# A transformer block on one core: memory keys and shared keys earlier, second values later

## The chip, the cores and the metric

One core of a Trainium2 chip runs the whole program as one launch. The metric is device time in microseconds (us) of one execution, input in device memory to output in device memory; lower is better. The core has five engines with an instruction queue each, worked through in order: TensorE (PE; its weight loads are listed as PEld), VectorE (DVE), ScalarE (ACT), GpSimd (POOL) and SyncE (SP), which here issues nearly all transfers (DMAs). DMAs move data between device memory and the on-chip memories; PSUM is the memory into which TensorE writes, in eight banks.

## What is computed

Chunked attention with memory keys and values, and then a mixture of eight experts in which each token goes to one expert. Cut to what matters:

```python
# B, H, S, D = 4, 8, 768, 64; 8 memory rows a head; chunks of 32 queries
for c in range(S // 32):
    q_c   = q[:, :, c_start:c_start + 32]
    k_ctx = k[:, :, max(0, c_start - 16):min(S, c_end + 8)]   # left 16, own 32, right 8
    v_ctx = v[:, :, same rows]
    k_full, v_full = concat([mem_k, k_ctx]), concat([mem_v, v_ctx])
    a = softmax(q_c @ k_full.T / sqrt(D))
    out[:, :, c_start:c_end] = a @ v_full
x = out as 3072 tokens of 512
expert = argmax(x @ w_gate); gate = softmax of it
y = relu(x_e @ w1[e]) @ w2[e] for each expert's tokens (at most `capacity`), times gate
```

## The kernel before

**Tiling.** The attention goes through 12 segments of 256 tokens (four batches of three) and 24 tiles `t` of 128 tokens, two to a segment `n`. For a segment, `load_k` and `load_q` (L360, L352) bring keys and queries of all eight heads with two tokens to a partition; `trans_k` and `trans_q` transpose them on TensorE; ACT and DVE copy the result from PSUM into the key window `KW` and into `qT`. The window has, for each chunk, 64 columns: 24 keys that it shares with the chunk before it, 32 own ones, 8 memory keys; heads come in pairs, so that a head's 64 rows stand in a half `hf` of the partitions and the other half's columns must be zero. `copy_k` fills the shared columns: L492 puts the first keys of a batch (from `preT`) into the first chunk, L496 copies the last 24 own keys of each chunk into the next, L498 into the next segment's window. `fill_mem_k` (L450) fills the memory columns from `preT`, which `trans_pre` makes out of one load of `mem_k` (L118) and one of the first keys (L119). Values come in blocks `k` of two tiles: `load_v` (eight heads, eight transfers and one small one), `fill_mem_v` (two transfers from the tile `ME` that GpSimd assembles from `mem_v`), `copy_v` (L414, L415).

**A tile.** `scores(t)`: 16 products on TensorE (L509, listed as 32 matmuls), a maximum (L517) and a subtraction (L520) on DVE. `exps(t)` on ACT (L526), `trans_p`, `value` (L550 on TensorE, L553 to L558 on DVE), `trans_out`, `logits`, and later `route`. Key windows and value windows have two buffers each (`KW[n % 2]`, `VW[k % 2]`), the raw loads a ring of two.

**Order.** Nothing is scheduled by a planner: each engine runs its instructions in the order in which the program writes them, and waits where a tile is not ready. Ahead of the loop stand the first loads, `dummy(11)` (each unit listed as two matmuls, on zeros), the zeroing of the windows (`zero_k`, `zero_v`, L128 and L135, both from a zero tile or as memset; L173 for one half of `KW[1]`), the first segment's transposes and copies, `dummy(20)`, the memory rows, the loads of segment 2 and of value block 1. In the loop, tile `t` of even number does `fill_mem_k(n)`, `scores`, `trans_k(n)`, `load_k(n + 2)` for `n = t // 2 + 1`; the odd tile does `scores`, `trans_q(n)`, `load_q(n + 2)`; then value work of the tiles before. Value block 2 and later ones are loaded from t = 3 on.

**SP's queue before**, in order: keys 0 (two halves), queries 0 (two halves), `mem_k`, first keys, `mem_v` of batch 0 (two), keys 1, queries 1, values 0 (nine), fill 0 (two), keys 2, queries 2, fill 1 (two), values 1 (eight), then from the loop `mem_v` of batch 1, keys 3, `w_gate`, `mem_v` of batch 2, queries 3, `mem_v` of batch 3, keys 4, queries 4, values 2 and so on.

The experts follow from about 137 us on: PE-bound matrix products with the weights split into two parts.

Of the kernel before, what the change touches and what calls it, by code (L numbers as in the profile page):

```python
# [17 lines left out]
P = 128  # L18
# [11 lines left out]
NKW, NVW = 2, 2  # L30
# [20 lines left out]
class Kernel:  # L51
# [41 lines left out]
    def attention(self):  # L93
# [31 lines left out]

        def zero_k(i, hf):
            r = slice(hf * 64, hf * 64 + 64)
            nc.vector.tensor_copy(out=KW[i][r, :, :, 1 - hf, :].rearrange("p a c d -> p (a c) d"),  # L128
                                  in_=self.pad[r, None, 0:64].broadcast_to([64, 32, 64]))
# [9 lines left out]

        self.load_k(0)  # L140
        self.load_q(0)
        load_mem()
        load_memv(0)
# [13 lines left out]
        zero_v(0, 0, nc.scalar.copy)  # L157
        zero_v(0, 1, None)
        self.load_v(0)
        self.trans_k(0)  # L160
        self.trans_q(0)
        self.trans_pre(pre)
        dummy(20)
        self.copy_k(0)
        self.fill_mem_k(0)
        zero_k(1, 0)
        nc.gpsimd.memset(ME, 0.0)
        for par in range(2):
            nc.gpsimd.memset(ME[par * 32:par * 32 + 32, par, :, 64:65], 1.0)
        for par in range(2):  # L170
            r = slice(par * 32, par * 32 + 8)
            nc.gpsimd.tensor_copy(out=ME[r, par, :, 0:64], in_=memv[r])
        nc.gpsimd.memset(KW[1][64:P, :, :, 0, :].rearrange("p a c d -> p (a c) d"), 0.0)  # L173
        self.fill_mem_v(0)
        self.load_k(2)
        self.load_q(2)
        zero_v(1, 0, None)
        zero_v(1, 1, None)
        self.fill_mem_v(1)
        self.load_v(1)  # L180
        self.okd = False
# [6 lines left out]
        for t in range(NTL):  # L188
# [12 lines left out]
            if n < NS:  # L201
                if t % 2 == 0:
                    self.trans_k(n)
                    if n + 2 < NS:
                        self.load_k(n + 2)
                else:
                    self.trans_q(n)
                    if n + 2 < NS:
                        self.load_q(n + 2)
            self.exps(t)  # L210
            if 0 <= t - 1 < NTL:
# [217 lines left out]
    def trans_pre(self, src):  # L429
# [5 lines left out]
        for j in range(2):  # L435
            for hf in range(2):
                nc.scalar.copy(out=self.preT[hf * 64:hf * 64 + 64, :, j::2, :].rearrange("p a r c -> p (a r) c"),
                                      in_=ps[j * 64:j * 64 + 64, hf::2].rearrange("p (a c) -> p a c", a=8))

# [3 lines left out]
    def fill_mem_k(self, n):  # L443
# [4 lines left out]
        for hf in range(2):  # L448
            r = slice(hf * 64, hf * 64 + 64)
            (self.nc.scalar.copy if n == 0 and not hf else (self.nc.gpsimd if n and not hf else self.nc.vector).tensor_copy)(  # L450
                out=kw[r, :, :, hf, 56:64], in_=self.pre_cols(0, b)[r, :, None, :].broadcast_to([64, 4, 8, 8]))
# [16 lines left out]
    def trans_k(self, n):  # L468
        nc = self.nc
        kw = self.KW[n % NKW]  # L470
        src = self.kn.pop(n)
        for hf in range(2):
            ps = self.psum().rearrange("p (h t) -> p h t", h=4)
            for i in range(4):
                nc.tensor.transpose(out=ps[:, i, :], in_=src[:, 2 * i + hf, :], identity=self.ident)
            ps = ps.rearrange("p h (m t) -> p h m t", t=16)
# [7 lines left out]
    def copy_k(self, n):  # L484

        nc = self.nc
        b, s = self.segs[n]
        kw, kx = self.KW[n % NKW], self.KW[(n + 1) % NKW]
        if s == 0:
            for hf in range(2):  # L490
                r = slice(hf * 64, hf * 64 + 64)
                nc.vector.tensor_copy(out=kw[r, :, 0, hf, 16:24], in_=self.pre_cols(1, b)[r])  # L492
        for hf in range(2):
# [560 lines left out]
```

## Time and profile before

| | us |
|---|---|
| median of 3 runs | 485.65 |
| the three runs | 484.39, 485.65, 493.61 |
| the profiled execution, its own time | 483.69 |
| span of the profiled execution, first to last instruction | 481.8 |
| busy in it: PE / DVE / ACT / POOL | 458.3 / 308.9 / 232.6 / 118.2 |

The 1.89 us between the span and the execution's own time lie around the program. Busy shares are means over an attention stage (to about 137 us) and an expert stage with different limits, so they are read by stage. A row of busy time by stretch gives the stretch, its length, the busy time of PE, PEld, DVE, ACT and POOL (each with the number of instructions), the clock granted to TensorE as a share of 2.4 GHz, the mean busy share of the sixteen DMA engines, and GB/s. A row of a timeline gives when a group of like instructions began, how long it lasted, engine, line, operation, out<-in with sizes, the count and, in brackets, how long the engine had sat idle before and what released it. An instruction that has been taken up but is blocked counts as busy, so an instruction that is longer than its twin tells of a wait.

### The profile page before, as it was taken

The numbers are of one execution on the slowest core, as the hardware profiler recorded it, in microseconds if no ns is written. First come the engines' busy times: TensorE is split into PE (matmuls) and PEld (weight loads), VectorE is DVE, ScalarE is ACT, GpSimd is POOL, SyncE is SP. The second block draws the span as 40 slices with busy tenths as digits, with TensorE's granted clock in tenths as the row PEclk, the third lists the DMA queues.
The fourth block names the chain that finished last, engine by engine and source line by source line (L and its number), as shares of the span: only waits on it lengthen the run. The fifth ranks groups of instructions, "written<-read, shape, count | busy, mean of one in ns | idle before, by whom it ended". The sixth has DMA issues, their size and how long they took to land.

```text
span 481.8 us, 11847 instructions
## 1 busy us (share of the span) xinstructions
PE 458.3 (95%) x4317; PEld 386.9 (80%) x4317; DVE 308.9 (64%) x686; ACT 232.6 (48%) x423; POOL 118.2 (25%) x158
## 2 busy tenths in 40 slices
PE   7899999999999999979999999999999999899993
PEld 6777877878789897867777898899888878677782
DVE  5988899999869447565448257555624676674410
ACT  6587968889635235255345056244502544533200
POOL 8631245555543621201001100100021011020011
PEclk9899999999999999999999999999999999999998
DMA  9787788897976755365705554270414356430011
GB/s 214 150 216 189 184 209 245 249 246 186 230 252 236 263 167 193 105 224 180 237 34 181 173 190 133 88 267 16 164 53 149 123 187 229 163 131 3 1 42 44
DMA packets 79920, 78.85 MB, mean 164 GB/s; under 512 B 33394, under 2 KB 60142, under 8 KB 79792
## 3 DMA queue, kind: packets, MB, share of 16 engines
q1 hardware_dynamic: 74992, 62.33, 44.4%
q0 software_dynamic: 4800, 14.95, 8.1%
q8 instruction: 65, 1.06, 1.0%
q14 instruction: 63, 0.52, 0.3%
HBM read 61.25 MB, written 15.99 MB: 160 GB/s over the span
## 4 chain that ended last, share of the span: by engine, by line
PE 52%; DMA 18%; issue 13%; DVE 10%; ACT 2%; SPq 1%; POOLq 1%; DVEq 0%; ACTq 0%
PE ps L858 19%; DMA out_dram<-y,tok 13%; PE ps L948 13%; PE lgp L927 5%; DMA raw<-in_q_dram 3%; PE ps L834 2%; PE ps L550 2%; DVE vw L415 2%; PE ps L463 2%; PE ps L509 2%; PE ps L331 2%; ACT kw L479 1%; DVE m L517 1%; DVE d L520 1%; SPq L397 1%
## 5 line engine op out<-in xcount | busy, mean ns | idle before, releaser
L871 ACT ACTIVATE hhi<-ps 128x512 fp32r<-128x512 f32 x68 | 40.7, 599 | 148.6 <-PE ps L858 133.0
L955 POOL DMA_INDIRECT out_dram<-y,tok x28 | 32.3, 1155 | 273.3 <-DVEq L842 140.9
L872 DVE SCALAR_TENSOR_TENSOR hlo<-ps,hhi 128x512 fp32r<-128x512 f32 x68 | 47.0, 691 | 68.6 <-ACT hhi L871 65.7
L858 PE MATMUL ps<-xhi,w1hi 128*128 128x320 f32 (+3 forms) x288 | 59.5, 328 | 3.6 <-ACT w2hi L849 1.7
L948 PE MATMUL ps<-w2hi,hhi 128*128 128x512 f32 x152 | 60.9, 401 | 0.0
L948 PE MATMUL ps<-w2lo,hhi 128*128 128x512 f32 x152 | 59.8, 393 | 0.0
L948 PE MATMUL ps<-w2hi,hlo 128*128 128x512 f32 x152 | 59.4, 391 | 0.0
L858 PE MATMUL ps<-xhi,w1lo 128*128 128x320 f32 (+3 forms) x288 | 57.7, 322 | 0.0
L858 PE MATMUL ps<-xlo,w1hi 128*128 128x320 f32 (+3 forms) x288 | 57.7, 322 | 0.0
L858 PEld LDWEIGHTS ps<-xhi,w1hi 128*128 128x128 f32 x288 | 45.2, 188 | 8.3 <-issue 2.1
L858 PEld LDWEIGHTS ps<-xhi,w1lo 128*128 128x128 f32 x288 | 45.9, 188 | 2.9
L858 PEld LDWEIGHTS ps<-xlo,w1hi 128*128 128x128 f32 x288 | 45.9, 188 | 2.8
L954 DVE TENSOR_SCALAR y<-ps,xg 128x512 f32<-128x512 f32 x19 | 14.3, 751 | 51.6 <-PE ps L948 44.0
L850 DVE TENSOR_TENSOR w2lo<-raw,w2hi 128x512 fp32r<-128x512 f32 x64 | 41.2, 685 | 0.9 <-DVEq L919 0.6
L823 DVE TENSOR_TENSOR w1lo<-raw,w1hi 128x512 fp32r<-128x512 f32 x56 | 36.7, 684 | 2.7 <-DVEq L842 0.8
L822 ACT CAST w1hi<-raw 128x512 fp32r<-128x512 f32 (+1 forms) x72 | 37.1, 573 | 0.9
L849 ACT CAST w2hi<-raw 128x512 fp32r<-128x512 f32 x64 | 36.2, 617 | 1.6 <-DMA raw<-in_moe_w_dram 1.6
L838 ACT CAST xhi<-ps 128x512 fp32r<-128x512 f32 x34 | 19.8, 587 | 29.6 <-PE ps L834 26.3
L948 PEld LDWEIGHTS ps<-w2hi,hlo 128*128 128x128 f32 x152 | 28.6, 188 | 6.7
L948 PEld LDWEIGHTS ps<-w2hi,hhi 128*128 128x128 f32 x152 | 28.5, 188 | 6.7
L839 DVE TENSOR_TENSOR xlo<-ps,xhi 128x512 fp32r<-128x512 f32 x34 | 23.1, 689 | 16.7 <-ACT xhi L838 16.7
L948 PEld LDWEIGHTS ps<-w2lo,hhi 128*128 128x128 f32 x152 | 28.5, 188 | 5.8
(169 smaller groups left out, 814.6 us busy)
## 6 DMA issues: line engine op xcount, KB each, us to landing
raw<-in_moe_w_dram SPq DMA_DIRECT2D x15, 2048.0 KB
raw<-in_q_dram SPq DMA_DIRECT2D x11, 512.0 KB
raw<-in_k_dram SPq DMA_DIRECT2D x10, 512.0 KB
vw<-in_v_dram SPq DMA_DIRECT2D x49, 64.0 KB
xg<-x_d SPq DMA_DIRECT2D x3, 792.0 KB
vw<-in_v_dram SPq DMA_DIRECT2D x31, 72.0 KB
xg<-x_d SPq DMA_DIRECT2D x4, 528.0 KB
xg<-x_d SPq DMA_DIRECT2D x2, 1056.0 KB
```

Of the source, the lines that this page charges most:

```text
L822: self.nc.scalar.copy(out=hi[sl], in_=raw[sl])
L823: (eng or self.nc.vector).tensor_tensor(out=lo[sl], in0=raw[sl], in1=hi[sl].bitcast(F32), op=ALU.subtract)
L838: nc.scalar.copy(out=self.xhi[:, d:d + k, sl], in_=pv)
L839: nc.vector.tensor_tensor(out=self.xlo[:, d:d + k, sl], in0=pv, in1=self.xhi[:, d:d + k, sl].bitcast(F32), op=ALU.subtract)
L849: self.nc.scalar.copy(out=self.w2a[:, j], in_=self.raw2[:, j])
L850: self.nc.vector.tensor_tensor(out=self.w2b[j // 4][:, j % 4], in0=self.raw2[:, j], in1=self.w2a[:, j].bitcast(F32), op=ALU.subtract)
L858: self.nc.tensor.matmul(ps, a[:, d, fs], b[:, d, o:o + w], start=(i + d == 0), stop=(i == 2 and d == KD - 1))
L871: self.nc.scalar.activation(out=self.hhi[hs], in_=ps, func=AF.Relu)
L872: self.nc.vector.scalar_tensor_tensor(out=self.hlo[hs], in0=ps, scalar=0.0, in1=self.hhi[hs].bitcast(F32), op0=ALU.max, op1=ALU.subtract)
L927: nc.tensor.matmul(ps, a, b, start=start, stop=stop)
L948: self.nc.tensor.matmul(ps, a[:, f, t * P:t * P + P], b, start=(f == 0 and i == 0), stop=(f == KF - 1 and i == 2))
L955: nc.gpsimd.indirect_dma_start(out=self.out[:, :], out_offset=bass.IndirectOffsetOnAxis(ap=tok[:, t:t + 1], axis=0), in_=y, in_offset=None ...
```

## The change

Ahead of the loop: `load_mem` goes before `load_q(0)`. `trans_k(0)` transposes the heads in the order in which the two halves of the load come. `copy_k` is split into `prior_k` (the first keys of a batch) and `share_k`; for segment 0 `share_k` comes right behind `trans_k(0)`, then `trans_pre`, `prior_k`, the memory rows of `ME`, `fill_mem_k(0)`, and only then `trans_q(0)`. Two of the four copies out of `trans_pre` go from ACT to DVE; the second copy of `fill_mem_k(0)` goes from DVE to POOL; `zero_k(1, 0)` goes from DVE to ACT. On POOL the memset of `KW[1]` comes first and `zero_v(0, 1)` last but two. `dummy(20)` becomes `dummy(4)`. On SP, fill 0 comes behind keys 2 and queries 2; values 1 and then fill 1 move into the loop at t = 1, behind keys 3 and queries 3. For segments 1 and up, `trans_k` asks for its two PSUM banks together and is otherwise as before.

```diff
@@ -123,9 +123,9 @@
                 nc.sync.dma_start(out=memv[par * 32 + b * 8:par * 32 + b * 8 + 8],
                                   in_=self.mem_v[b].rearrange("(r u) m d -> u m r d", u=2)[par])
 
-        def zero_k(i, hf):
+        def zero_k(i, hf, copy=nc.vector.tensor_copy):
             r = slice(hf * 64, hf * 64 + 64)
-            nc.vector.tensor_copy(out=KW[i][r, :, :, 1 - hf, :].rearrange("p a c d -> p (a c) d"),
+            copy(out=KW[i][r, :, :, 1 - hf, :].rearrange("p a c d -> p (a c) d"),
                                   in_=self.pad[r, None, 0:64].broadcast_to([64, 32, 64]))
 
         def zero_v(i, par, copy):
@@ -138,8 +138,8 @@
             nc.gpsimd.memset(VW[i][r, :, par, :, 64:65], 1.0)
 
         self.load_k(0)
+        load_mem()
         self.load_q(0)
-        load_mem()
         load_memv(0)
         self.load_k(1)
         self.load_q(1)
@@ -155,29 +155,28 @@
         nc.vector.memset(KW[0][:, :, 0, :, 0:24], 0.0)
         nc.vector.memset(VW[0][32:48, 0, 0, 0, 0:64], 0.0)
         zero_v(0, 0, nc.scalar.copy)
-        zero_v(0, 1, None)
         self.load_v(0)
-        self.trans_k(0)
-        self.trans_q(0)
-        self.trans_pre(pre)
-        dummy(20)
-        self.copy_k(0)
-        self.fill_mem_k(0)
-        zero_k(1, 0)
+        nc.gpsimd.memset(KW[1][64:P, :, :, 0, :].rearrange("p a c d -> p (a c) d"), 0.0)
         nc.gpsimd.memset(ME, 0.0)
         for par in range(2):
             nc.gpsimd.memset(ME[par * 32:par * 32 + 32, par, :, 64:65], 1.0)
+        self.trans_k(0)
+        self.share_k(0)
+        self.trans_pre(pre)
+        self.prior_k(0)
         for par in range(2):
             r = slice(par * 32, par * 32 + 8)
             nc.gpsimd.tensor_copy(out=ME[r, par, :, 0:64], in_=memv[r])
-        nc.gpsimd.memset(KW[1][64:P, :, :, 0, :].rearrange("p a c d -> p (a c) d"), 0.0)
-        self.fill_mem_v(0)
+        self.fill_mem_k(0)
+        self.trans_q(0)
         self.load_k(2)
         self.load_q(2)
+        dummy(4)
+        zero_k(1, 0, nc.scalar.copy)
+        zero_v(0, 1, None)
+        self.fill_mem_v(0)
         zero_v(1, 0, None)
         zero_v(1, 1, None)
-        self.fill_mem_v(1)
-        self.load_v(1)
         self.okd = False
         self.puts, self.routes, self.done = [], [], set(range(len(GROUPS)))
         ends = {t0 + w - 1: g for g, (t0, w) in enumerate(GROUPS)}
@@ -207,6 +206,9 @@
                     self.trans_q(n)
                     if n + 2 < NS:
                         self.load_q(n + 2)
+            if t == 1:
+                self.load_v(1)
+                self.fill_mem_v(1)
             self.exps(t)
             if 0 <= t - 1 < NTL:
                 self.trans_p(t - 1)
@@ -434,8 +436,9 @@
                                 identity=self.ident[0:32, 0:32])
         for j in range(2):
             for hf in range(2):
-                nc.scalar.copy(out=self.preT[hf * 64:hf * 64 + 64, :, j::2, :].rearrange("p a r c -> p (a r) c"),
-                                      in_=ps[j * 64:j * 64 + 64, hf::2].rearrange("p (a c) -> p a c", a=8))
+                (nc.vector.tensor_copy if hf else nc.scalar.copy)(
+                    out=self.preT[hf * 64:hf * 64 + 64, :, j::2, :].rearrange("p a r c -> p (a r) c"),
+                    in_=ps[j * 64:j * 64 + 64, hf::2].rearrange("p (a c) -> p a c", a=8))
 
     def pre_cols(self, kind, b):
         return self.preT[:, kind, :, 4 * b:4 * b + 4].rearrange("p r c -> p c r")
@@ -447,7 +450,7 @@
             return
         for hf in range(2):
             r = slice(hf * 64, hf * 64 + 64)
-            (self.nc.scalar.copy if n == 0 and not hf else (self.nc.gpsimd if n and not hf else self.nc.vector).tensor_copy)(
+            (self.nc.scalar.copy if n == 0 and not hf else (self.nc.gpsimd if not n or not hf else self.nc.vector).tensor_copy)(
                 out=kw[r, :, :, hf, 56:64], in_=self.pre_cols(0, b)[r, :, None, :].broadcast_to([64, 4, 8, 8]))
 
     def trans_q(self, n):
@@ -469,10 +472,11 @@
         nc = self.nc
         kw = self.KW[n % NKW]
         src = self.kn.pop(n)
-        for hf in range(2):
-            ps = self.psum().rearrange("p (h t) -> p h t", h=4)
-            for i in range(4):
-                nc.tensor.transpose(out=ps[:, i, :], in_=src[:, 2 * i + hf, :], identity=self.ident)
+        pss = [self.psum().rearrange("p (h t) -> p h t", h=4) for _ in range(2)]
+        for h in range(H):
+            hf, i = (h % 2, h // 2) if n == 0 else (h // 4, h % 4)
+            nc.tensor.transpose(out=pss[hf][:, i, :], in_=src[:, 2 * i + hf, :], identity=self.ident)
+        for hf, ps in enumerate(pss):
             ps = ps.rearrange("p h (m t) -> p h m t", t=16)
             r = slice(hf * 64, hf * 64 + 64)
             for j in range(2):
@@ -483,13 +487,22 @@
 
     def copy_k(self, n):
 
+        self.prior_k(n)
+        self.share_k(n)
+
+    def prior_k(self, n):
+
         nc = self.nc
         b, s = self.segs[n]
-        kw, kx = self.KW[n % NKW], self.KW[(n + 1) % NKW]
         if s == 0:
             for hf in range(2):
                 r = slice(hf * 64, hf * 64 + 64)
-                nc.vector.tensor_copy(out=kw[r, :, 0, hf, 16:24], in_=self.pre_cols(1, b)[r])
+                nc.vector.tensor_copy(out=self.KW[n % NKW][r, :, 0, hf, 16:24], in_=self.pre_cols(1, b)[r])
+
+    def share_k(self, n):
+
+        nc, s = self.nc, self.segs[n][1]
+        kw, kx = self.KW[n % NKW], self.KW[(n + 1) % NKW]
         for hf in range(2):
             r = slice(hf * 64, hf * 64 + 64)
             copy = nc.scalar.copy if n == 0 and not hf else (nc.vector if n <= 1 or hf else nc.gpsimd).tensor_copy
```

## Rows read from the trace of the kernel before

**Rows 1.** Busy time of the engines in three stretches of the span

```profile
0.00:17.00 17.00, 12.74 (x158) 10.83 (x162) 11.95 (x16) 8.87 (x14) 14.86 (x22) 0.93 0.82 181
17.00:42.00 25.00, 24.28 (x477) 20.20 (x469) 22.71 (x56) 20.76 (x35) 6.79 (x21) 0.98 0.80 197
42.00:137.00 95.00, 91.36 (x1863) 74.55 (x1862) 86.48 (x271) 75.16 (x140) 45.45 (x71) 1.00 0.84 217
```

**Rows 2.** Timeline of DVE to 26 us

```profile
1.18 2.46 DVE L128 COPY kw<-pad 64x2048 f32<-64x2048 f32 x2
...
10.09 2.63 DVE L492 COPY kw<-preT 64x32 f32<-64x32 f32 x2 [0.74 <-ACT preT L437]
...
13.51 3.04 DVE L128 COPY kw<-pad 64x2048 f32<-64x2048 f32 x1
...
17.17 0.69 DVE L517 TENSOR_REDUCE m<-ps 128x8 f32<-128x512 f32 x1
...
19.97 0.68 DVE L517 TENSOR_REDUCE m<-ps 128x8 f32<-128x512 f32 x1
...
25.10 0.51 DVE L496 COPY kw<-kw 64x672 f32<-64x672 f32 x1 [0.77 <-ACT kw L479]
```

**Rows 3.** Timeline of POOL to 18 us

```profile
7.90 0.84 POOL L172 COPY ME<-memv 8x256 f32<-8x256 f32 x2 [1.12 <-DMA memv<-in_mem_v_dram]
...
10.64 2.05 POOL L135 MEMSET vw<- 64x2340 f32 x1
...
13.23 2.23 POOL L135 MEMSET vw<- 64x2340 f32 x1
...
16.71 0.71 POOL L450 COPY kw<-preT 64x256 f32<-64x256 f32 x1
```

**Rows 4.** Timeline of ACT to 19 us

```profile
2.04 2.14 ACT L137 COPY vw<-pad 64x2340 f32<-64x2340 f32 x1
...
9.25 1.09 ACT L437 COPY preT<-ps 64x128 f32<-64x128 f32 x4 [1.06 <-PE ps L433]
...
10.37 0.75 ACT L496 COPY kw<-kw 64x672 f32<-64x672 f32 x1
...
15.85 2.52 ACT L479 COPY kw<-ps 64x512 f32<-64x512 f32 x4 [4.03 <-PE ps L475]
```

**Rows 5.** Timeline of PE to 23 us

```profile
6.42 2.19 PE L463 MATMUL ps<-ident,raw 128*64 128x128 f32 x32 [0.95 <-DMA raw<-in_q_dram]
...
13.63 1.14 PE L509 MATMUL ps<-kw,qT 128*32 128x128 f32 x32 [1.93 <-DVE kw L450]
...
14.70 1.97 PE L475 MATMUL ps<-ident,raw 128*128 128x128 f32 x8
...
21.73 1.09 PE L475 MATMUL ps<-ident,raw 128*128 128x128 f32 x8
```

**Rows 6.** Busy time in the stretch of the lower granted clock

```profile
14.50:18.00 3.50, 3.50 (x44) 2.87 (x40) 3.39 (x5) 2.10 (x4) 3.44 (x9) 0.51 0.71 131
```

**Rows 7.** Timeline of SP's queue to 39 us

```profile
6.40 1.43 SPq L397 DMA_DIRECT2D vw<-in_v_dram  x1
...
16.74 2.24 SPq L426 DMA_DIRECT2D vw<-ME  x2
...
19.04 6.22 SPq L397 DMA_DIRECT2D vw<-in_v_dram  x8
...
31.08 7.57 SPq L397 DMA_DIRECT2D vw<-in_v_dram  x8
```

**Rows 8.** Timeline of PE and DVE around tiles 4 and 5

```profile
31.90 1.13 PE L550 MATMUL ps<-vw,pT 128*32 128x130 f32 x32
...
35.69 0.23 DVE L553 TENSOR_SCALAR rc<-ps 128x4 f32<-128x4 f32 x2
...
42.32 0.69 DVE L415 COPY vw<-vw 24x768 f32<-24x768 f32 x1 [0.67 <-issue]
```

**Rows 9.** The chain that ended last, in order of time: start, duration, work

```profile
91.20 8.55 DMA raw<-in_q_dram
```

## The prediction

> **What bounds the kernel now.** I read the busy time by stage first: after the first 17 us DVE is busy for 22.71 of 25 us and then for 86.48 of 95 us, while the DMA engines stand at 0.80 and 0.84 [rows 1]. The attention stage to 137 us is thus paced by DVE, with TensorE (24.28, 91.36) waiting inside its busy time and the loads close behind. Before 17 us DVE is not full (11.95 of 17), and the change works there. So the question is when DVE's steady work begins, and what it meets afterwards.
>
> DVE's timeline says when: the maximum of tile 0 (L517) starts at 17.17, that of tile 1 at 19.97 [rows 2]. The products of tile 0 had begun at 13.63 [rows 5] and take 1.14, so DVE and not TensorE is late by 2.4 us. What stood in front is the zeroing L128, 3.04 us, although two such copies took 2.46 at the start of the kernel, 1.23 each [rows 2]. POOL's timeline gives the reason: a memset runs from 13.23 to 15.46, and L128, taken up at 13.51, ends 1.1 us after it. Likewise the two tiny copies L492 take 2.63 us until the memset of 10.64 to 12.69 is over [rows 2, 3]. So a DVE copy inside SBUF and a POOL instruction take turns, each for its whole length, and DVE gets in between two POOL instructions. This decides most of the sum.
>
> The products of tile 0 are at 13.63 because they waited 1.93 us for the last copy into the key window [rows 5], which waits for `preT`: its four copies run on ACT at 9.25 to 10.34, after TensorE did the queries first [rows 4, 5].
>
> **The change part by part.**
>
> *Load order.* Two transfers of 64 KB go ahead of the queries. Their cost lies between nothing (if the DMA engines have room) and 131 KB at the stage's 181 GB/s, 0.7 us [rows 1]; I take 0.7, because TensorE already waited for the queries (0.95 us idle, then 6.42) [rows 5]. The queries' transposes then start at 7.1, last 2.19, and end at 9.3; a DVE pass over 128x512 (0.69, as L517) gives `qT` at 10.0. The `mem_v` loads keep their place.
>
> *Key window.* The shared copies (0.75 on ACT for the large one [rows 4]) and `preT` (1.09 for four on one engine, so about 0.55 on two) move into the time in which TensorE waits for queries; they cost nothing as long as they end before 10.0. `preT` on DVE is not in the trace; bounds are 0.27 (ACT's) and 0.69 a copy, and either ends before 9. The second memory copy, now on POOL, comes after L172 (7.90 to 8.74 [rows 3], it waits for `mem_v`) and takes 0.71, so 9.45. Tile 0's products therefore start at about 10.0 and end at 11.15: 3.6 us earlier. Order of the heads in `trans_k(0)`: between 0 and a few tenths, hidden by the same wait for queries; I take 0. The pair of PSUM banks asked for together costs nothing: the transposes keep their order.
>
> *Zeroing on ACT.* L128 leaves DVE (3.04). On ACT it is 2.14 x 2048/2340 = 1.87 by L137 [rows 4], in a place where ACT had idled for 4.03 us before L479. Hidden; if ACT had no room, it would cost its 1.87 there.
>
> *Tile 0 on DVE.* In front of the maximum one SBUF copy is left (L450 for segment 1). POOL now runs `zero_v(0, 1)` behind its memory copy, 9.45 to 11.5 at 2.05 [rows 3]. L450 waits for its end and the maximum starts at about 12.1, not 17.17: 5.1 us earlier.
>
> *Tile 1 on DVE.* The four shared copies of segment 1 stand behind tile 0's subtraction (13.5). POOL's two other memsets of 2.05 run from 12.0 on. Taking turns: first copy 14.05 to 14.55, second to 14.9, the next memset 14.9 to 16.95, third and fourth copy to 17.8. Tile 1's maximum starts at 17.8, not 19.97: 2.2 us earlier. So the memsets that were moved back take more than half of the gain.
>
> *Segment 2.* POOL's copy L450 of segment 1 (0.71) comes after all that, at 17.8 to 18.5, against 16.71 to 17.42 [rows 3]. Tile 2's products need it, so TensorE, done with tile 1 and the transposes of segment 1, stands idle from about 15.7 (an estimate) to 18.5. Then 1.1 for the products, half of the transposes (0.55), four ACT copies of 0.63 (2.52 [rows 4]): done at 23.0, and DVE's copy L496, which had waited 0.77 us for ACT until 25.10 [rows 2], is 2.1 us earlier. That is at the full clock. At the lower one the same transposes took 1.97 instead of 1.09 [rows 5], in a stretch with a granted clock of 0.51 (1.2 GHz) which began within a microsecond after an idle time of 1.93 us [rows 5, 6]. With the longer idle of 2.8 us and the dummies cut to a fifth, I expect this: about 0.6 for the products and 0.2 to 0.4 for half of the transposes more, and L496 is 1.4 us earlier. Between 1.4 and 2.1 I take 1.7.
>
> The Trainium skill says in "TensorE: Matmul & The Clock Gate", section "Part 1: The HAM clock gate (the "warmup" mystery)", that "the default state is throttled, and activity releases the throttle", which speaks against taking dummies away. The trace agrees with a clock of 0.51 after the idle time [rows 6]; by the rule alone this term would be 1.4, without it 2.1.
>
> *SP's queue.* The transfers are the same, in another order. The first value load went out at 6.40, when the first queries landed (TensorE took them up at 6.42), although it needs nothing of them [rows 5, 7]: SP lets a transfer go when the eighth before it has landed. Before, fill 1 cost 2.24 us at 16.74 (it waits for POOL), then eight value loads 6.22, all ahead of keys 3 and queries 3. After, those two go at about 17.3 and 20.7, values 1 from about 21 (the eighth before the first is fill 0) to 25 to 27, fill 1 until 26.7 to 28.9, keys 4 and queries 4, then values 2 at about 30.5 instead of 31.08. The last of values 2 held DVE for 0.67 us at 42.32 [rows 8], 11.2 us after the first was issued [rows 7], since the four loads of keys and queries 3 and 4 (512 KB each) lay right ahead of it. Two of them now go ahead of values 1, whose issue alone takes 6.22 us. Gain 0 to 0.67; I take 0.3.
>
> *Sum.* 1.7 + 0.3 = 2.0 us off. The stage behind is DVE's at 91% [rows 1], so a shift of DVE's start should stay. Profiled execution: 483.69 - 2.0 = 481.7. The profiled execution lies 1.96 below the median of the runs, which contains 493.61; the mean of 483.69, 484.39 and 485.65 is 484.6, and from this I forecast 482.6.
>
> **The rivals.**
>
> *Larger gain: POOL and DVE do not hold each other up so.* POOL alone would need 9.45 + 3 x 2.05 + small ones, and finish L450 at 16.7. Segment 2's copies would be done at 21.3: 3.8 us earlier, with the 0.67 up to 4.5. Time 480.1 to 480.8. Against it stand both pairs of rows of DVE and POOL [rows 2, 3].
>
> *No change: the loads give the pace.* If values 2 land when they did, L415 is at 42.32 again and all is as before: 484.6. For it: SP is a queue of unchanged transfers, and a value block took 6.22 and 7.57 us to issue [rows 7]. Against: DMA engines at 0.80 between 17 and 42 us [rows 1], and the gap is what keys 3 and queries 3 move into. It decides if values 2 start after 31 and need their 11 us.
>
> *Slower: fill 1 lands late.* It now stands behind values 1 and goes out at about 27.5 instead of 16.74; tile 2's value products need it. They ran at 31.90 and DVE read them at 35.69, so there are 2.7 us of slack [rows 8]. How long a fill takes under load is not in the trace; the ends are nothing beyond its issue (2.24 for two [rows 7]) and 8.55, the longest load on the chain [rows 9]. At 8.55 the products start at 36.1, 4.2 us late, less 2.7 of slack: 1.5 us slower at first, up to 4.2 if tile 5's products behind them on TensorE are late too: 486.1 to 488.8. It decides from a landing of about 7 us on. The same holds for fill 0, now behind keys 2 and queries 2, due at 21.
>
> **How the numbers follow.** Forecast (1 to 3 us off) 0.45, larger gain 0.15, no change (within 1 us) 0.25, slower 0.15. The forecast's own range is 481.6 to 483.6. The 8 in 10 reaches over half of the larger gain and over a third of the slower case and takes in about 1 us by which the runs shown scatter: 479.5 to 487.0. Two per cent, about what a measurement of this kernel can tell from no change, is 9.7 us. The sum of all credits, 5.1 at tile 0 and 0.67, is not that, and neither is the slower end, 4.2 with 1 us of clock: faster 0.01, same 0.96, slower 0.03.
>
> **What would show it.** Right: tile 0's maximum near 12, tile 1's near 18, DVE's third shared copy blocked until a memset of POOL ends, the lower clock between 18 and 22, no idle of DVE before L415 of tile 4. Wrong: L550 of tile 2 or of tile 0 waiting for a fill; L415 again at 42.3; tile 1's maximum before 16. What would make it wrong most easily is the load side, whose times I only bounded.

## The result and the profile after

The changed kernel is slower by 1%: the median over 13 runs is 489.48 us (486.67 to 494.9), that of the kernel before, run beside it as often, 484.71 us (482.45 to 493.61). The ratio is 1.0101, with a 95% interval of 1.0071 to 1.0131, so between 3.4 and 6.3 us were lost. The forecast was 482.6 us, with a range to 487.0. The profiled execution of the changed kernel took 491.59 us (span 489.80), 2.1 us above its own median; that of the kernel before took 483.69 (span 481.8).

Line numbers behind the change have moved: L417 is the former L415, L466 L463, L478 L475, L500 L492, L509 L496, L522 L509, L530 L517, L563 L550, L871 L858, L880 L867.

Busy time of the engines by stage in the kernel after (stretch, its length, then busy us and instructions of PE, PEld, DVE, ACT, POOL, then the granted clock, the DMA engines' share and GB/s):

```profile
0.00:17.00 17.00, 12.62 (x152) 10.47 (x152) 13.24 (x20) 11.28 (x15) 14.09 (x23) 0.90 0.70 176
17.00:42.00 25.00, 21.49 (x404) 17.92 (x400) 18.82 (x46) 18.45 (x30) 6.85 (x21) 0.93 0.81 182
42.00:137.00 95.00, 91.15 (x1872) 74.73 (x1870) 86.53 (x265) 75.38 (x139) 44.99 (x71) 1.00 0.85 216
137.00:489.80 352.80, 335.35 (x1874) 286.19 (x1865) 189.56 (x358) 128.48 (x239) 50.75 (x45) 0.98 0.42 144
```

Against [rows 1], DVE is busier before 17 us (13.24 for 11.95; a part is time in which it was held up, below) and less between 17 and 42 (18.82 for 22.71: it waits there). The last row is a stage that the change does not touch: 352.80 us from 137 us on. Before it was 481.8 - 137 = 344.8; 2.1 of the 8.0 us between them were there before the first stop in the experts, as the table at the end of this section shows.

The start, first on DVE (start, duration, engine, line, operation, tiles, and in brackets the idle time ahead):

```profile
9.24 2.80 DVE L500 COPY kw<-preT 64x32 f32<-64x32 f32 x2
12.06 0.69 DVE L468 COPY qT<-ps 128x512 f32<-128x512 f32 x1
...
14.47 0.69 DVE L530 TENSOR_REDUCE m<-ps 128x8 f32<-128x512 f32 x1
...
17.31 0.77 DVE L509 COPY kw<-kw 64x672 f32<-64x672 f32 x1 [0.34 <-ACT kw L483]
...
18.31 0.68 DVE L530 TENSOR_REDUCE m<-ps 128x8 f32<-128x512 f32 x1
...
23.74 0.51 DVE L509 COPY kw<-kw 64x672 f32<-64x672 f32 x1 [1.07 <-ACT kw L483]
...
30.52 0.68 DVE L417 COPY vw<-vw 24x768 f32<-24x768 f32 x1 [0.94 <-DMA vw<-ME]
...
38.37 0.69 DVE L530 TENSOR_REDUCE m<-ps 128x8 f32<-128x512 f32 x1
```

and on POOL:

```profile
9.27 0.63 POOL L453 COPY kw<-preT 64x256 f32<-64x256 f32 x1 [0.62 <-DVE preT L439]
9.84 2.05 POOL L135 MEMSET vw<- 64x2340 f32 x1
...
16.96 0.61 POOL L453 COPY kw<-preT 64x256 f32<-64x256 f32 x1
```

and on ACT:

```profile
14.76 2.52 ACT L483 COPY kw<-ps 64x512 f32<-64x512 f32 x4 [2.81 <-PE ps L478]
```

Tile 0's maximum (L530) is at 14.47 for 17.17, tile 1's at 18.31 for 19.97, segment 2's copy (L509) at 23.74 for 25.10 [rows 2]: 2.7, 1.7 and 1.4 us earlier. Then the gain is lost: tile 5's maximum, at 37.87 before, is at 38.37. PE and SP's queue show by what:

```profile
12.18 1.50 PE L522 MATMUL ps<-kw,qT 128*32 128x128 f32 x32 [2.78 <-DVE kw L500]
...
34.08 1.96 PE L563 MATMUL ps<-vw,pT 128*32 128x130 f32 x32 [3.00 <-DVE d L533]
```

```profile
22.63 6.66 SPq L399 DMA_DIRECT2D vw<-in_v_dram  x8
29.33 1.47 SPq L428 DMA_DIRECT2D vw<-ME  x2
```

Tile 2's value products (L563) stand 3.00 us idle, 2.2 us later than before [rows 8]. The row names DVE's L533, the subtraction of tile 4, which these products don't need: in after_dummy20 (below) they start at 32.33, ahead of tile 4's maximum at 32.53. What TensorE's queue had to wait for was fill 1 (`vw<-ME`), issued from 29.33 on, with its second half landing at 33.95. The lower clock follows (the number behind the seven busy times):

```profile
33.50:37.00 3.50, 2.92 (x36) 2.25 (x36) 2.77 (x10) 2.27 (x3) 2.68 (x8) 0.51 0.82 230
```

The larger loss is elsewhere, in the expert stage. TensorE at two places of it, first after, then the same two places before:

```profile
207.66 0.72 PE L871 MATMUL ps<-xhi,w1hi 128*128 128x256 f32 x4 [0.25 <-DVE hlo L885]
208.22 0.64 PE L871 MATMUL ps<-xhi,w1lo 128*128 128x256 f32 x4
208.69 0.28 PE L871 MATMUL ps<-xlo,w1hi 128*128 128x256 f32 x1
211.50 1.01 PE L871 MATMUL ps<-xlo,w1hi 128*128 128x256 f32 x3 [2.53 <-issue]
...
377.88 0.33 PE L880 MATMUL ps<-pad 128*64 128x64 f32 x2
381.32 1.06 PE L871 MATMUL ps<-xhi,w1hi 128*128 128x320 f32 x4 [3.11 <-DVEq L921]
```

```profile
205.52 0.71 PE L858 MATMUL ps<-xhi,w1hi 128*128 128x256 f32 x4 [0.25 <-DVE hlo L872]
206.07 0.63 PE L858 MATMUL ps<-xhi,w1lo 128*128 128x256 f32 x4
206.54 0.64 PE L858 MATMUL ps<-xlo,w1hi 128*128 128x256 f32 x4
...
214.07 0.33 PE L867 MATMUL ps<-pad 128*64 128x64 f32 x2 [1.67 <-issue]
...
373.55 0.33 PE L867 MATMUL ps<-pad 128*64 128x64 f32 x2
373.80 0.85 PE L858 MATMUL ps<-xhi,w1hi 128*128 128x320 f32 x4
```

Up to 207.66 the changed kernel is 2.14 us late. There TensorE stops after the first of four like matmuls (`xlo,w1hi`), which read slices of the same two tiles, and the trace lists no semaphore wait ahead of the second: no result of another engine is missing. "issue" says that the profile shows no wait. The second stop, 3.11 us behind the two `pad` matmuls, does not exist before, where 373.55 is followed at once by 373.80. The kernel before has a stop of this kind too, 1.67 us at 212.40, but a smaller one.

The DMA queues of the kernel after, around each stop, in the stretches 209.0 to 209.2 and 378.6 to 378.8 (packets, MB, share of the DMA engines):

```profile
q8 instruction: 1, 0.02, 27.5%
...
q8 instruction: 1, 0.02, 30.0%
```

The queue "instruction" moves pieces of 16 KB (65 packets and 1.06 MB in either kernel). One piece starts just behind each stop, and TensorE goes on 2.4 and 2.6 us later. The code of the experts has branches on the number of tokens (`tc.If` in line L902), and the second stop falls into one: a compare-and-branch of TensorE's sequencer, which works ahead of the matmuls, begins at 375.7 and takes 5.32 us, where the median of those between 371.6 and 387.4 is 0.18.

```profile
L902 PEldq COMPARE_BRANCH  x1: 5323/5323/5323, 375.7 to 375.7; - x1
```

And each stop is followed by the lower clock:

```profile
211.00:214.50 3.50, 3.00 (x14) 3.00 (x15) 0.69 (x1) 0.60 (x1) 0.00 (x0) 0.51 0.82 300
...
381.50:385.00 3.50, 3.50 (x15) 3.50 (x15) 0.00 (x0) 0.45 (x1) 0.00 (x0) 0.53 0.11 37
```

Counting TensorE's matmuls back from the last one gives stretches of equal work in both kernels. The table holds the start of the matmul that has so many behind it, in us, and the difference of the two profiled executions:

| matmuls still to come | 1420 | 1300 | 560 | 440 | end of span |
|---|---|---|---|---|---|
| before | 202.95 | 224.17 | 363.64 | 383.28 | 481.79 |
| after | 205.09 | 228.25 | 367.97 | 391.71 | 489.80 |
| difference | 2.14 | 4.08 | 4.33 | 8.43 | 8.02 |

So of the 8.0 us between the two executions, 2.1 are there with 1420 matmuls to come (2.6 with 1870 to come, near the end of the attention stage: 136.84 for 134.21), 1.9 come from the stretch of the first stop and 4.1 from that of the second; the rest of the stage takes as long as before.

### The profile page after: what moved, and what is told of

Same layout as the page of the kernel before. It is cut to its first block, busy times and chain, and to the rows that moved or that the text cites. A ratio compares the mean times of both kernels' runs of the same rounds, so it can differ in the third digit from the quotient of the medians.

```text
span 489.8 us, 11779 instructions
## 1 busy us (share of the span) xinstructions
PE 460.6 (94%) x4285; PEld 389.3 (79%) x4285; DVE 308.1 (63%) x686; ACT 233.6 (48%) x422; POOL 116.7 (24%) x159
## 3 DMA queue, kind: packets, MB, share of 16 engines
q8 instruction: 65, 1.06, 0.9%
## 4 chain that ended last, share of the span: by engine, by line
PE 55%; DMA 17%; issue 14%; DVE 10%; SPq 1%; ACT 1%; POOLq 1%; DVEq 0%; ACTq 0%
PE ps L871 19%; DMA out_dram<-y,tok 13%; PE ps L961 13%; PE lgp L940 5%; PE ps L563 3%; PE ps L522 3%; PE ps L847 2%; PE ps L466 2%; DVE vw L417 2%; DMA vw<-ME 2%; PE ps L333 1%; PE ps L618 1%; PE ps L478 1%; DVE m L530 1%; DMA raw<-in_q_dram 1%
## 5 line engine op out<-in xcount | busy, mean ns | idle before, releaser
L871 PE MATMUL ps<-xhi,w1hi 128*128 128x320 f32 (+3 forms) x288 | 60.4, 332 | 5.6 <-DVEq L921 3.1
L871 PE MATMUL ps<-xlo,w1hi 128*128 128x320 f32 (+3 forms) x288 | 59.1, 327 | 2.5 <-issue 2.5
L871 PE MATMUL ps<-xhi,w1lo 128*128 128x320 f32 (+3 forms) x288 | 58.6, 326 | 0.0
L871 PEld LDWEIGHTS ps<-xhi,w1hi 128*128 128x128 f32 x288 | 46.3, 192 | 9.9 <-issue 5.1
L871 PEld LDWEIGHTS ps<-xlo,w1hi 128*128 128x128 f32 x288 | 47.1, 193 | 5.6 <-issue 2.7
L871 PEld LDWEIGHTS ps<-xhi,w1lo 128*128 128x128 f32 x288 | 46.8, 192 | 2.9
L563 PE MATMUL ps<-vw,pT 128*32 128x130 f32 x768 | 28.6, 283 | 6.5 <-DVE d L533 3.0
L483 ACT COPY kw<-ps 64x512 f32<-64x512 f32 x46 | 28.5, 620 | 10.6 <-PE ps L478 9.2
```

What stands on the lines that cost most here:

```text
L483: (nc.vector.tensor_copy if n == 0 and hf else nc.scalar.copy)(out=kw[r, :, :, hf, 24 + j:56:2], in_=ps[j * 64:j * 64 + 64])
L563: nc.tensor.matmul(ps[32 * c4:32 * c4 + 32, i * 130:i * 130 + 130], pT[:, pr * P + 32 * c4:pr * P + 32 * c4 + 32], vw[:, c + c4 + 1, :, pr ...
L871: self.nc.tensor.matmul(ps, a[:, d, fs], b[:, d, o:o + w], start=(i + d == 0), stop=(i == 2 and d == KD - 1))
```

## The experiments

Two theories stood at first. One: the late fill 1 and the wait at tile 2 cost the time (the prediction's own slower rival). Two: the sixteen units that `dummy(4)` has less than `dummy(20)` cost it, since every instruction behind them stands elsewhere in TensorE's program. The first four kernels ran on one chip beside 29 runs of the kernel before (median 485.34); the next four (before_dummies_moved, after_dummies_moved, after_dummy12 and after_dummy20_fill_first; median before 497.10, 35 runs) and the last four (499.75, 29 runs) on two others, which are slower for every kernel. A ratio is taken within the rounds of one such group, so it can differ a little from that of the medians, and the ratios rather than the times are compared across groups.

**The changed kernel with twenty units again** (after_dummy20):

```
-        dummy(4)
+        dummy(20)
```

> The changed kernel with 20 dummy units instead of 4 in the same place, so that TensorE runs as many instructions as before the change. Late fill (fill 1 lands too late for tile 2's value products, a wait of 3.0 us there): 3 us slower than the kernel before, about 488, the wait at tile 2 still there. Moved code (32 matmuls fewer shift where TensorE's instruction transfers fall, so that it stands idle 2.5 us near 209 and 3.1 us near 378 us in the expert stage): those two idle times go, 2 to 3 us faster than the changed kernel, about 486.5. The lower clock at 13 us should go in either case, since the idle time of 2.8 us before it is filled.

Measured: 484.33 us, ratio to before 0.9948 (0.9915 to 0.9981). With the units back, the rest of the change is a gain: 2.5 us by the ratio, 1.0 by the medians. The step from the changed kernel is about twice the 2 to 3 us that were expected. Its tiles 0 and 1 have their maxima at 14.24 and 18.16. TensorE at the place of the first stop and at tile 2:

```profile
32.33 1.10 PE L563 MATMUL ps<-vw,pT 128*32 128x130 f32 x32 [2.02 <-DMA vw<-ME]
...
207.59 0.64 PE L871 MATMUL ps<-xlo,w1hi 128*128 128x256 f32 x4
209.44 0.71 PE L871 MATMUL ps<-xhi,w1hi 128*128 128x256 f32 x4 [1.21 <-ACT w2hi L862]
...
213.73 0.33 PE L880 MATMUL ps<-pad 128*64 128x64 f32 x2 [1.21 <-issue]
```

The wait for fill 1 is there (2.02 us) and the time is a gain nonetheless. The stops are where the kernel before had its own, and short.

**Only the dummies cut, in the kernel before** (before_dummy4):

```
-        dummy(20)
+        dummy(4)
```

> The kernel before with 4 dummy units instead of 20 and nothing else. Late fill: no change, 484.7 within 1 us, no idle time of 2 us or more in the expert stage. Moved code: 2 to 3 us slower, with idle times near 207 and 375 us beside a transfer of TensorE's instructions. A start held up by a longer lower clock would cost under 1 us, as DVE is late there anyway.

Measured: 491.32 us, ratio 1.0115 (1.0084 to 1.0147). This single number in a kernel without any reordering costs 5.6 us, twice what was expected, and gives both stops of the changed kernel. TensorE:

```profile
13.94 1.94 PE L509 MATMUL ps<-kw,qT 128*32 128x128 f32 x32 [4.28 <-DVE kw L450]
...
208.01 0.28 PE L858 MATMUL ps<-xlo,w1hi 128*128 128x256 f32 x1
210.25 0.62 PE L858 MATMUL ps<-xlo,w1hi 128*128 128x256 f32 x3 [1.96 <-issue]
...
377.26 0.33 PE L867 MATMUL ps<-pad 128*64 128x64 f32 x2
380.53 1.41 PE L858 MATMUL ps<-xhi,w1hi 128*128 128x320 f32 x4 [2.94 <-DVEq L908]
```

It stops after the first of the four `xlo,w1hi`, and behind the two `pad`, as the changed kernel does. The lower clock at the start (4.28 us without work instead of 1.93, then 1.94 for products that took 1.14 [rows 5]) leaves it 0.9 us late with 1870 matmuls to come (135.16 for 134.21); 1.5 are reached with 1420 to come (204.43 for 202.95), and the stretches of the two stops cost 1.84 and 5.14 more.

**Only values 1 and fill 1 late, in the kernel before** (before_values_late):

```
-        self.fill_mem_v(1)
-        self.load_v(1)
...
+            if t == 1:
+                self.load_v(1)
+                self.fill_mem_v(1)
```

> The kernel before with only one move: values 1 and then fill 1 go behind keys 3 and queries 3 at tile 1. Late fill: tile 2's value products wait 2 us or more for the fill and the kernel is 2 to 3 us slower than before (487 to 488). Moved code: no change (TensorE's instructions are the same), 484.7.

Measured: 486.21 us, ratio 1.0007 (0.9983 to 1.0032). Tile 2's products stand idle 1.61 us, up to 32.93, and the kernel is 1.1 us late at 1420 matmuls to come; in the median 0.9 us are left of that, within the interval of nothing. Alone this move gives 0.3% at most, not 1%.

**Values 1 and fill 1 early, in the changed kernel** (after_values_early):

```
+        self.fill_mem_v(1)
+        self.load_v(1)
...
-            if t == 1:
-                self.load_v(1)
-                self.fill_mem_v(1)
```

> The changed kernel with fill 1 and values 1 back ahead of the loop, in this order. Late fill: the wait of 3.0 us goes, tile 4's maximum is at about 31 instead of 32.6, and the attention stage ends 1.5 to 2 us before that of the kernel before; the time falls by 3 to 4 us, to about 485.5 if the idle times of the expert stage stay, and to 483 if they don't. Moved code: time falls by 1 us or less.

Measured: 489.44 us, ratio 1.0085 (1.0057 to 1.0113). The wait at tile 2 is gone, and it is nearly as slow as the changed kernel. TensorE:

```profile
31.87 1.10 PE L562 MATMUL ps<-vw,pT 128*32 128x130 f32 x32
...
208.91 0.98 PE L870 MATMUL ps<-xlo,w1hi 128*128 128x256 f32 x4 [2.10 <-issue]
...
377.88 0.82 PE L870 MATMUL ps<-xhi,w1hi 128*128 128x320 f32 x4 [2.48 <-DVEq L920]
```

Tile 2 is now at 31.87 without idle time, where it was before [rows 8], while both stops remain. The wait for fill 1, the one thing in the attention stage that looks like the culprit, is not where the 1% lies: the two ratios differ by 0.16%, 0.8 us, and by their intervals it could be nothing or up to 2.8 us.

**The sixteen units moved, not removed** (before_dummies_moved, after_dummies_moved). In the kernel before sixteen units go ahead of the queries' transposes, in the changed kernel behind `share_k(0)`:

```
         self.trans_k(0)
+        dummy(16)
         self.trans_q(0)
         self.trans_pre(pre)
-        dummy(20)
+        dummy(4)
```

```
         self.share_k(0)
+        dummy(16)
         self.trans_pre(pre)
```

> The kernel before with its 20 dummy units split: 16 go ahead of the queries' transposes, 4 stay. TensorE runs the same number of instructions as before, and what follows tile 0 stands where it stood, but TensorE is idle for 3 us or more ahead of tile 0 and its clock falls, as with 4 units alone. Code position: as the kernel before, 484.5 to 486, transfers of TensorE's instructions near 206 and 375 us, no idle time of 2 us at 208 or 378. Clock or idle time at the start: as with 4 units, 490 to 491.

> The changed kernel with 16 more dummy units, between the shared keys and the transposes of the memory rows, 4 staying where they are. Code position: the gain of the version with 20 units, 484 to 485, although the lower clock near 13 us can come back. Clock at the start: as the changed kernel, 489.

Measured: 497.48 us, ratio 1.0038 (1.0001 to 1.0075), and 495.34 us, ratio 0.9981 (0.9942 to 1.0020). TensorE still stands idle ahead of tile 0 (3.38 and 1.87 us, against 4.28 and 2.78 without the sixteen units), and the lower clock follows in before_dummies_moved (0.52 from 15.0 to 18.5 us), though not in after_dummies_moved (1.00 from 6 to 20 us). The program ahead of the experts is as long as with twenty: the loss shrinks from 1.15% to 0.4%, and the changed kernel is no longer slower. The 0.4% that stays in before_dummies_moved fits the idle time and the clock at the start; no run separates these. What separates 0.9981 from the 0.9948 of after_dummy20 was not settled; the chips differ and the intervals overlap.

**Twelve units in the changed kernel** (after_dummy12, `dummy(12)`):

> The changed kernel with 12 dummy units, half way. Clock: the idle time ahead of tile 0 is about 1.8 us, so close to the version with 20. Code position: every unit shifts what follows, and the late transfers of instructions near 208 and 378 us get earlier with the count: between the two, 485.5 to 488, with idle times there of 1 to 2 us.

Measured: 501.94 us, ratio 1.0057 (1.0011 to 1.0102). TensorE stops at yet another place:

```profile
214.95 0.63 PE L871 MATMUL ps<-xlo,w1hi 128*128 128x256 f32 x4
218.26 0.47 PE L880 MATMUL ps<-pad 128*64 128x64 f32 x2 [2.67 <-issue]
```

A stop of 2.67 us is still there, some ten matmuls earlier in the program than with four units, and the longest near the second place is 1.03 us. So half the units don't make half the stops, as was expected; they move them.

**Sixty-eight units, in both kernels** (after_dummy68, before_dummy68; `dummy(68)`). The trace lists a unit as two matmuls and two weight loads, so 64 more units are 256 instructions. The Trainium skill, "Trainium Architecture — The Big Picture", section "The software stack", gives an instruction 64 bytes; by that, as an estimate, the 64 units fill just one piece of 16 KB, and every instruction behind lies where it lies with four units. The traces agree: the two versions with 68 units move 66 pieces, all others 65.

> The changed kernel with 68 dummy units. A dummy unit is listed as two matmuls and two weight loads; if each is 64 bytes of program, 64 units fill one 16 KB transfer of instructions, so that 68 units put all that follows where 4 units put it. Code position, in the sum of TensorE's idle times in the expert stage: as with 4 units (idle times of over 2 us near 208 and 378 us plus the later start), 2 to 4 us more than with 20 units. Any other account (more dummies keep the clock up, the start is covered): the idle times stay as with 20 units. The start itself costs about 5 us (64 units at 0.118, less the idle time of 2.8), so the time is 491 to 495 on a chip where the kernel before takes 485.

> The kernel before with 68 dummy units, the place in the program of the version with 4. Code position: idle times of over 2 us in the expert stage, as with 4 units, on top of a start later by some 4 us: 1.5 to 2.2% slower. Otherwise: the later start alone, 0.8% slower, idle times as in the kernel before.

Measured: 504.02 us, ratio 1.0079 (1.0037 to 1.0122), and 505.67 us, ratio 1.0149 (1.0089 to 1.0208). The 64 units themselves take TensorE's time at the start, so the ratios alone say little; the places say more. The queue "instruction" in the whole of before_dummy68, and TensorE there:

```profile
q8 instruction: 66, 1.08, 0.9%
```

```profile
226.73 0.64 PE L858 MATMUL ps<-xlo,w1hi 128*128 128x256 f32 x4 [2.06 <-issue]
...
396.48 0.82 PE L858 MATMUL ps<-xhi,w1hi 128*128 128x320 f32 x4 [2.58 <-DVEq L908]
```

Both stops are back, in a kernel with 48 units more than the one that has neither. Counted from the end of TensorE's list, the stops of 1.0 us and more behind the matmul with 1420 to come (idle us in brackets; the same stop can fall one matmul earlier or later; some kernels have stops ahead of 1420 as well, such as 1.76 us at 1635 in after_dummy12, which are left out):

| kernel | units | matmuls to come at the stops |
|---|---|---|
| before | 20 | 1354 (1.67), 288 (1.74) |
| before_values_late | 20 | 1378 (1.25), 1354 (1.20), 288 (1.84) |
| after_dummy20 | 20 | 1378 (1.21), 1354 (1.21), 288 (1.88), 264 (1.16) |
| after_dummy20_fill_first | 20 | 1354 (1.50), 288 (1.86), 264 (1.19) |
| after_dummy20_zero_early | 20 | 1378 (1.27), 288 (1.72) |
| after_dummy20_zero_early_fill | 20 | 1378 (1.12), 1354 (1.32), 288 (1.64) |
| before_dummies_moved | 16 + 4 | 1378 (1.11), 1354 (1.56), 288 (1.64), 264 (1.40) |
| after_dummies_moved | 16 + 4 | 1378 (1.01), 1354 (1.32), 288 (1.88) |
| after | 4 | 1393 (2.53), 498 (3.11), 288 (1.42) |
| before_dummy4 | 4 | 1393 (1.96), 1344 (1.28), 498 (2.94), 288 (1.58) |
| after_values_early | 4 | 1394 (2.10), 498 (2.48), 288 (1.35), 264 (1.00) |
| after_dummy68 | 68 | 1394 (2.67), 498 (2.31), 288 (1.07), 264 (1.25) |
| before_dummy68 | 68 | 1394 (2.06), 498 (2.58), 288 (1.41), 264 (1.26) |
| after_dummy12 | 12 | 1404 (2.68), 474 (1.03), 288 (1.02), 264 (1.42) |

The long stops go by the number of units, whichever kernel it is and wherever the units stand ahead: 1393 and 498 with 4 and with 68, neither with 20. The stop at 288 is in all of them and makes no difference.

**Versions with twenty units that mend the order** (after_dummy20_fill_first: fill 1 ahead of values 1; after_dummy20_zero_early: `zero_v(0, 1)` back right behind `zero_v(0, 0)`; after_dummy20_zero_early_fill: both). The two edits on top of `dummy(20)`:

```
             if t == 1:
-                self.load_v(1)
                 self.fill_mem_v(1)
+                self.load_v(1)
```

```
         zero_v(0, 0, nc.scalar.copy)
+        zero_v(0, 1, None)
...
-        zero_v(0, 1, None)
         self.fill_mem_v(0)
```

> The changed kernel with 20 dummy units and, at tile 1, fill 1 ahead of values 1. The wait of 2.0 us for fill 1 at tile 2's value products (at 32 us with 20 units) goes. Late fill costs time that stays: 1 to 1.5 us faster than with 20 units alone, 483. Slack or loads take it up: no difference (484.3).

> The changed kernel with 20 dummy units and the zeroing of value window 0 back at its early place on POOL, so that only two long memsets are left behind POOL's memory copy. Turns between DVE and POOL: POOL's copy of the memory keys of segment 1 ends near 15 instead of 17.4 us, tile 1's maximum is 1 to 2 us earlier than at 18.2; time 1 us less than with 20 units alone, 0.6 to 0.8% under the kernel before. Dummies or ACT's copies late next: no difference (0.5% under).

> As the one before, and fill 1 ahead of values 1 at tile 1. If fill 1 is what holds tile 2's value products after the earlier start, 1 us less again, 0.8 to 1% under the kernel before; if the loads take it back in the tiles after, no difference to the one before.

Measured: 495.82 us, ratio 0.9974 (0.9937 to 1.0012); 495.70, ratio 0.9940 (0.9900 to 0.9981); 496.40, ratio 0.9973 (0.9932 to 1.0015). Fill 1 ahead of values 1 gives nothing that can be seen, though with both edits tile 2's products start without a wait. The early zeroing beats the kernel before by 0.6%, as after_dummy20 does by 0.5%; which of the two is better the intervals don't tell. POOL's copy for segment 1 ends at 15.45 there, as expected, but tile 1's maximum is at 17.82 for 18.16, not 1 to 2 us earlier: it did not hang on POOL. Tile 2's products in after_dummy20_zero_early wait 0.47 us for the fill, at 31.44, and tile 4 has its maximum at 31.50 for 32.35 before:

```profile
31.44 1.11 PE L563 MATMUL ps<-vw,pT 128*32 128x130 f32 x32 [0.47 <-DMA vw<-ME]
```

## Why the prediction was wrong

**The step that failed** is the term of the dummies: "the dummies cut to a fifth" stood in the sum as part of 0.7 us between two values of segment 2's copy, a matter of the clock before 23 us. Alone it costs 1.15%, 5.6 us. Most of that lies in a stage that the prediction did not look at: 1.84 and 5.14 us at the two stops of before_dummy4, 1.9 and 4.1 in the changed kernel. It is idle time and the lower clock behind it, in about equal parts: in the changed kernel 2.53 and 3.11 us idle, less the 1.67 and 0.72 that the kernel before stands idle in the first of these stretches, make 3.3; twice 3.5 us at about half the clock cost 1.7 each. Together 6.7, where the two stretches show 6.0.

**What makes the stops.** Shown: removing sixteen units makes the two long ones, putting them back anywhere ahead removes them, and one piece of 16 KB more brings them back. Shown as well, though the trace names no engine for the queue: the pieces are TensorE's code, and TensorE waits for them. Only the versions with 68 units, which differ from the others in TensorE's list alone, move a 66th piece. In the fourteen traces 138 compare-and-branch instructions of TensorE's sequencer took over 1.0 us, and each ended 2.3 to 2.9 us after a piece had begun to move; in each of the 44 stops of the table TensorE went on 2.3 to 2.8 us after one. What differs is when the piece starts: in the stops of 1.9 us and more from 0.4 us before the stop to 0.5 behind it (209.11 for 208.97 and 378.67 for 378.21 in the changed kernel, 206.54 for 206.81 in after_values_early), in the shorter ones 0.8 to 1.7 us before it. The branches also fit that it is the experts' stage: up to 137 us the kernel before brings in 20 pieces for 4978 matmuls and weight loads, after it 45 for 3661, so much of the code that is brought in there seems to be jumped over. Open: why a piece is not asked for sooner at these places. Around both stops the DMA engines are full (1.01 of their time from 207 to 211 us, 1.02 from 378 to 381.5), but before, where the pieces come ahead of the need, they are at 0.99 from 203 to 207 and at 0.83 from 374 to 378; experts' weights loaded at other times were not tried.

**The rest of the sum had the right sign, and its size by luck.** 2.0 us was forecast for the order, and after_dummy20 is ahead by 0.52% (0.2 to 0.85%): 2.5 us, or 1.0 by the medians. With the 5.6 of before_dummy4 that makes a loss of 3.1 to 4.6, where 4.9 was measured. But the forecast's path, an earlier start of DVE that stays, is not what the trace of after_dummy20 shows. Segment 2's copy is 1.94 us earlier there (23.16 for 25.10), and tile 4's maximum is later than before (32.53 for 32.35), since DVE stands idle 1.69 us for fill 1 up to 30.50. With 1870 matmuls to come it is 0.9 us ahead, and the two profiled spans are alike (482.0 and 481.8). Where the gain of the medians is made is not shown.

**Step by step.**

- Tile 0: its products were to start at 10.0 and started at 12.18 (13.63 before). The prior keys' copies on DVE (L500), taken for free, lie in front: two copies of 64x32 took 2.80 us, from 9.24 until a memset of POOL from 9.84 to 11.89 was over (0.71 in after_dummy20). The queries' pass (L468) and the maximum came behind them, at 12.06 and 14.47 instead of 10 and 12.1. The turn-taking of DVE and POOL was the prediction's own mechanism [rows 2, 3]; it failed to apply it to the smallest copies on the list.
- The Trainium skill, "SBUF — State Buffer", section "Who interferes with whom", says that a DVE copy in its two-port mode and a GpSimd instruction lock each other out for a whole instruction. The measured 2.80 us for two small copies agrees; that DVE always gets in between two POOL instructions, as the prediction had it, does not hold: the second copy, taken up at 9.45, waited through the end of a POOL copy (9.27 to 9.90) and the whole memset.
- Tile 1: forecast 17.8, measured 18.31. Segment 2's copy: forecast 1.4 to 2.1 us earlier, measured 1.36. Both were met by luck. The forecast had them hang on POOL's last memset, which was to block DVE's third shared copy, with TensorE idle from 15.7 to 18.5 us. In the trace POOL's copy for segment 1 is early (16.96 instead of 17.8), that third copy waits for ACT (0.34 us, up to 17.31), ACT for segment 1's transposes, and TensorE works without a pause from tile 0's products at 12.18 up to 22.0. So both hang on tile 0, which was 2.2 us late, and on the lower clock, which came at 13.5 to 17.0 (0.57) and not between 18 and 22. The prediction's own terms for segment 2 add up to 22.7 (18.5 + 1.1 + 0.55 + 2.52), not to its 23.0.
- Values 2 were to be issued at 30.5 instead of 31.08; their first load stands in SP's queue at 33.90. The block of values 1, its fill and keys 4 and queries 4 took longer than the bounds allowed.
- The slower rival came true in its mechanism: fill 1, forecast for 27.5, was issued at 29.33, and tile 2's products were 2.2 us late (34.08 for 31.90 [rows 8]). Its price (1.5 to 4.2 us) did not: before_values_late is 0.9 us above before in the medians, and undoing the move in the changed kernel takes 0.16% off the ratio, 0.8 us (with an interval from nothing to 2.8). The profiled execution of the changed kernel is 2.1 us late with 1420 matmuls to come, that of after_values_early 0.1 (203.05 for 202.95); how much of the difference is the wait and how much the clock of 0.51 behind it was not separated. The rival's sign was right by another cause.
- "The stage behind is DVE's at 91% [rows 1], so a shift of DVE's start should stay" did not hold in the attention stage (1.4 us earlier at segment 2's copy, 0.5 late at tile 5's maximum), and it left out the experts, whose 344.8 us make up 72% of the span.

## What to carry to other kernels

A dead instruction ahead of a long program with branches is not only time and warmth where it stands: it sets where all code behind it lies, so change the count of instructions and the order in separate steps, or keep the count while the order is judged. Where a stage that a change does not touch becomes longer, line both traces up from the end of an engine's instruction list and look for idle time in the middle of a run of like instructions, marked "issue", for a compare-and-branch that takes microseconds, and for a transfer of the instruction queue beside them. The longest new wait in a profile (3.00 us at tile 2) may be worth little: only undoing it alone says so.

## What the runs showed of the hardware

- TensorE stopped for 1.0 to 3.1 us at places that go by the number of instructions ahead of them, the same places for 4 and for 68 units. It went on 2.3 to 2.8 us after a transfer of 16 KB of its instructions had begun, in all 44 stops of the table; up to 137 us, where the kernel before has one branch of TensorE's sequencer (at 132.1), 20 such transfers were needed, behind that, with 190 branches, 45.
- An idle time of some 2.5 us does not decide the clock. In the profile of after_values_early, 2.10 us at 206.81 were followed by the lower clock and 2.48 us at 375.40 were not:

```profile
208.50:212.00 3.50, 3.09 (x15) 3.09 (x15) 0.69 (x1) 0.60 (x1) 0.00 (x0) 0.57 0.89 319
377.50:381.00 3.50, 3.12 (x21) 3.15 (x22) 0.70 (x2) 0.60 (x1) 0.00 (x0) 1.00 0.42 150
```

The granted clock is the number behind the seven busy times and counts: 0.57 (mostly 1.2 GHz) in the first stretch, 1.00 (2.4 GHz) in the second. So the price of a stop varies by some 1.7 us (half of 3.5) with what the clock does behind it. The Trainium skill, "TensorE: Matmul & The Clock Gate", section "Part 1: The HAM clock gate (the "warmup" mystery)", says that the number of slow matmuls is run-variable, with examples from a kernel's start. The traces agree for a place in the middle of a kernel: behind the first stop the clock was 0.51 in the changed kernel, 0.57 in after_values_early and 1.00 in before_dummy4 (210.0 to 213.5), after 2.53, 2.10 and 1.96 us without work.
